# Two MLPs behind an RWKV-7 scan on one core: a new cost model for the planner, a gate on either of two engines, two interleaved blocks

## The chip, the cores and the metric

The kernel runs on one core of a Trainium2 chip. The time is device microseconds from the start of the execution to its end; of several runs the median is taken. The engines are TensorE (PE; its weight loads are shown apart as PEld), VectorE (DVE), ScalarE (ACT), GpSimd (POOL) and SyncE (SP), which here issues all DMAs. Each works through its own list of instructions in a fixed order and waits on semaphores where an input comes from another one.

## The reference

Attention is a recurrence over 768 tokens for 4 x 8 heads of size 40, followed by two MLPs over 3072 tokens with 320 features and 2048 hidden units, each with a squared Relu:

```
for t in range(S):
    y[:, :, t] = einsum('bhd,bhde->bhe', rt, state)
    Sa = einsum('bhde,bhe->bhd', state, at)
    state = state * wt[:, :, None, :] - einsum('bhd,bhe->bhde', Sa, bt)
    state = state + einsum('bhd,bhe->bhde', vt, kt)
x = y as (3072, 320)
x = relu(x @ moe_w_in) ** 2 @ moe_w_out
return relu(x @ moe2_w_in) ** 2 @ moe2_w_out
```

## The kernel before

**Attention** is done in chunks of 32 tokens. There are 12 units of 64 tokens and two halves of the batch, so 24 slots. For two slots at a time `keys` and `invert` prepare the chunk's triangular system: four scans of 520 elements along the decays, transposes on VectorE, and a long chain of small VectorE operations. `values` and `chain` then carry the state from chunk to chunk with many small matmuls in fp32.

**The MLPs** work in 12 blocks of 256 tokens, each in 16 steps `f` of 128 hidden units. A step is an `in_step` (8 matmuls of 256 columns into one of two banks `HB`), a `gate`, and an out step. In the first MLP (`block1`, `out_step1`) the out step has 8 matmuls of 256 columns; in the second (`block2`, `out_step2`) 6 of 320. Values are split into a high and a low part in fp32r, so that three products stand for one: the gate makes Relu (into `m_r`, which lies in the tile `mm`), the square of it, the rounded high part `m_h` and the rest `m_l`. Relu and Square are ScalarE's; `copy(AV, ...)` may go to ScalarE or VectorE, `sub(VG, ...)` to VectorE or GpSimd. `m_h` and `m_l` are rings of three, `m_r` and `HB` of two. The first MLP's block can start when both slots of its unit are done; it is the filler of TensorE during attention.

**The weights** come as 64-bit numbers and are decoded into pairs of fp32r by `halves` and `decode_t` (first MLP, beside the first slots) or `decode` (second MLP, when attention has ended and its memory is free). `halves` has three VectorE operations on U32. The second MLP needs slice `f` of its weights for step `f` of block 0.

**The order** of all of this is worked out by a planner (`_Plan`). Each operation is recorded with its inputs, its outputs and a priority (a lower number goes first): gate -200 and up, blocks' input -100 and up, attention by its slot's number, decoding 2.7, MLP matmuls 1000 and up. `run` simulates the five engines with the durations of `cost` (`array` and `pe_time` for TensorE), always takes the engine that can start first (in a tie VectorE, then ScalarE, GpSimd, TensorE, SyncE), and emits the operation in that order. An operation recorded by `either` goes to the engine that takes it first, but VectorE at first passes over one that another engine would end no more than `BIAS` = 800 ns later (lines 352 to 355). If nothing else is left for it and nothing is due within 300 ns, VectorE takes it all the same (lines 361 to 365). The planner's durations are thus not the chip's; only the order and the engine that it chose are what runs. `self.left` counts the operations with a tag that are still to be emitted; attention's have the tag "att".

An out step of the MLPs has the priority of its in step plus 1.5, so TensorE does in(j), out(j-1), in(j+1), out(j), and a gate has the time of out(j-1) and in(j+1) to finish. `check_w` (16 reductions over the decays, after the fourth block) looks for decays outside a range, for which a general version stands at the end of the program; it doesn't run with these inputs.

Every operation of the planner shows line 69 in the profile, so groups are told apart by their tiles.

Of the kernel before, what the change touches and what calls it, by code (L numbers as in the profile page):

```python
# [26 lines left out]
NF = 16  # L27
# [45 lines left out]
class _Plan:  # L73
# [65 lines left out]
    def cost(self, eng, op, outs, ins):  # L139
        o = outs[0]  # L140
        n = 1
        for _, c in o.ap[1:]:
            n *= c
        if eng == "SP":
            return 690.0 if o.ap[0][1] in (32, 64) else 480.0
        psum = any(str(z.space).endswith("PSUM") for z in ins)
        if eng == "ACT":
            return (55 if psum else 93) + (90 if len(ins) > 1 else 0) + n / 1.2
        if eng == "POOL":
            return 149 + 2.1 * n if ins else 35 + 0.83 * n  # L150
        if op == "reciprocal":
            return 70 + n * 6.25
        if op == "tensor_reduce":
            n = 1
            for _, c in ins[0].ap[1:]:
                n *= c
        if op in ("tensor_copy", "tensor_scalar") and not psum:
            n /= 2
        return (64 + n) / 0.96

# [87 lines left out]
    def array(self, ops):  # L248

        cycles, columns, tiles, mode = 0, 0.0, [], None  # L250
        for _, _, passes, outs, ins, _ in ops:
            k, m = ins[0].ap[0][1], ins[0].ap[1][1]
            n = 1
            for _, c in outs[0].ap[1:]:
                n *= c
            r0, c0 = ins[0].offset // ins[0].ap[0][0], outs[0].offset // outs[0].ap[0][0]
            rows = 32 if k <= 32 else 64 if k <= 64 else 128
            cols = 32 if m <= 32 else 64 if m <= 64 else 128
            if rows == 128:
                r0 = 0  # L260
            mode = (rows, cols)
            if ins[0].dtype == F32R:
                cycles += max(n, 2 * m) + 6
                columns += n * m / 128
                tiles = []
                continue
            tile_ = (r0, c0)
            clash = [z for z in tiles if not (z[0] != r0 or z[1] != c0)] or (
                rows == 128 and any(z[1] == c0 for z in tiles)
            )  # L270
            if tiles and not clash:
                cycles += passes / 2 * m
                columns += passes * n * m / 128
                tiles.append(tile_)
            else:
                cycles += passes * max(n, m)
                columns += passes * n * m / 128
                tiles = [tile_]
        return mode, cycles, columns
# [40 lines left out]
    def run(self, until=None):  # L320
        while until is None or self.left.get(until, 0):
# [20 lines left out]
            if e == "DVE":  # L342
                keep = []
                while avail:
                    z = heapq.heappop(avail)
                    j = z[1]
                    if j in self.done:
                        continue
                    keep.append(z)
                    alts = self.tasks[j][0]  # L350
                    cost = alts[e][1]
                    if any(
                        max(self.free[o], self.ready[j][o], t) + alts[o][1] <= t + cost + BIAS for o in alts if o != e
                    ):
                        continue
                    i = j
                    keep.pop()
                    break
                for z in keep:
                    heapq.heappush(avail, z)  # L360
                if i is None and self.pend[e] and self.pend[e][0][0] < t + 300:
                    self.free[e] = self.pend[e][0][0]
                    continue
# [24 lines left out]
def rwkv7_two_mlp_kernel(  # L388
# [611 lines left out]

    def gate(h, i):
        gg, gh, gl = m_r[i % 2], m_h[i % NG], m_l[i % NG]
        A.activation(out=gg, in_=h, func=AF.Relu)
        A.activation(out=gg, in_=gg, func=AF.Square)
        copy(AV, gh, gg)
        sub(VG, gl, gg, gh.bitcast(F32))

# [84 lines left out]

    obs = [bank[0:2], bank[2:4]]

    def block2(m, at, rows):
        ob = obs[m % 2]
        plan.prio = P_X + m
        load_x(x2a[at].rearrange("p (k t) -> p k t", k=2), x2b[at])
        split_x(m_xh[m % 2], m_xl[m % 2])
        for f in range(NF):  # L1100
            i = m * NF + f
            j = NBLK * NF + i
            plan.prio = P_M + j
            in_step(w2, m_xh[m % 2], m_xl[m % 2], f, HB[i % 2][:, 0:256])
            plan.prio = P_G + j
            gate(HB[i % 2][:, 0:256], i)
            plan.prio = P_M + j + 1.5
            out_step2(w2, f, i, ob)
        plan.prio = P_G + j
        for s in range(2):  # L1110
            o = m_o[s]
            src = ob[s][:, 0:320]
# [27 lines left out]
        V.tensor_reduce(out=wrow[:, 256:257], in_=wrow[:, 0:256], axis=AX.X, op=ALU.max)  # L1140
        V.tensor_copy(out=wbad, in_=wrow[:, 256:257])

    for m in range(NBLK):
        block2(m, m, lambda p, s: orow[p, s, m])
        if m == min(3, NBLK - 1):
            check_w()
    plan.run()
    sched.__exit__(None, None, None)
# [45 lines left out]
    with tc.If(bad > 0):  # L1194
# [3 lines left out]
        plan.run()  # L1198
        with tc.For_i(0, NU) as q:
            block1(0, q)  # L1200
            block2(0, q, lambda p, s: orow[p, s, bass.ds(q, 1)].rearrange("o t d -> (o t) d"))
            plan.run()
        w2x.close()

# [77 lines left out]
```

## Time and profile before

| | |
|---|---|
| median of 3 runs | 1204.93 us (1204.58 to 1208.73) |
| profiled execution | 1209.43 us, span 1207.6 us |
| mean granted TensorE clock | 0.955 |
| busy TensorE, VectorE, ScalarE, GpSimd | 1104.0, 805.9, 747.5, 388.2 us |

The page's second part shows the span in 40 slices of 30.2 us; a digit is the busy share in tenths. [...] A list of waits names the waiting engine and what it wrote to, then the engine and the tile that released it, the sum of the waits, their number and the longest. A group of instructions has the output and input tiles, the shape, the count, the busy time, the mean duration in ns, and the engine's idle time just before them.

### The profile page before, as it was taken

How to read it: one execution, taken by the hardware profiler on the slowest of the kernel's cores; microseconds unless marked ns; L12 is line 12 of the kernel's file. 1: busy time of each engine (PE TensorE's matmuls, PEld its weight loads, DVE VectorE, ACT ScalarE, POOL GpSimd, SP SyncE). 2: the span in 40 equal slices, each digit the busy share in tenths (PEclk: the TensorE clock that was granted, in tenths of full speed). 3: DMA queues.
4: the chain of work that ended last, by engine and by line, in shares of the span. 5: the costliest groups of instructions: out<-in, count | busy, mean ns of one | idle time of the engine just before them, and what ended most of it. 6: DMA issues, size and time to landing. Idle time of an engine off the chain costs nothing.

```text
span 1207.6 us, 43193 instructions
## 1 busy us (share of the span) xinstructions
PE 1104.0 (91%) x18096; PEld 1032.2 (85%) x18096; DVE 805.9 (67%) x1786; ACT 747.5 (62%) x2077; POOL 388.2 (32%) x443
## 2 busy tenths in 40 slices
PE   3888898998989998899899999999899999999996
PEld 2656787887878887798789899999899999999996
DVE  6887888789888978999798746666773232222221
ACT  4496554555565565556446468888666666666664
POOL 7544334223323332343224117776820000000000
PEclk9986789999998999999899999999899999999999
DMA  8555343155325515533451322332241010101000
GB/s 244 143 154 146 85 104 103 57 127 146 79 70 138 136 49 127 143 90 78 123 121 36 60 74 84 93 93 82 79 140 36 25 29 24 33 24 27 13 12 14
DMA packets 142239, 103.86 MB, mean 86 GB/s; under 512 B 98001, under 2 KB 110162, under 8 KB 142034
## 3 DMA queue, kind: packets, MB, share of 16 engines
q1 hardware_dynamic: 142034, 101.00, 31.5%
q8 instruction: 144, 2.36, 0.8%
q14 instruction: 61, 0.50, 0.1%
HBM read 82.88 MB, written 11.80 MB: 78 GB/s over the span
## 4 chain that ended last, share of the span: by engine, by line
PE 50%; DVE 7%; ACT 3%; issue 2%; DMA 1%; POOL 1%; SPq 1%; DVEq 0%; ACTq 0%; POOLq 0%
PE bank L69 50%; DVE mm L69 3%; DVE q L69 2%; ACT mm L69 1%; ACT q L69 1%; SPq L69 1%; DVE x L69 0%; DVE y L69 0%; DVE kt L69 0%; ACT m_h L69 0%; DMA v<-in_el_dram 0%; POOL kb L69 0%; DMA lk<-kt 0%; DVE p L69 0%; DMA mm<-in_win_dram 0%
## 5 line engine op out<-in xcount | busy, mean ns | idle before, releaser
L69 PE MATMUL bank<-m_xh,wi 128*128 128x256 f32 x1920 | 387.0, 286 | 9.7 <-ACT mm L69 5.4
L69 POOL TENSOR_TENSOR m_l<-mm,m_h 128x256 fp32r<-128x256 f32 x200 | 162.8, 816 | 546.3 <-ACT m_h L69 293.7
L69 PEld LDWEIGHTS bank<-m_xh,wi 128*128 128x128 f32 x1920 | 315.3, 193 | 13.2 <-ACT mm L69 6.0
L69 PE MATMUL bank<-m_xl,wi 128*128 128x256 f32 x1152 | 324.2, 285 | 1.8 <-POOL m_xl L69 1.8
L69 ACT ACTIVATE mm<-bank 128x256 f32<-128x256 f32 x384 | 146.2, 382 | 233.1 <-PE bank L69 214.3
L69 DVE TENSOR_TENSOR m_l<-mm,m_h 128x256 fp32r<-128x256 f32 x184 | 85.0, 462 | 217.6 <-ACT m_h L69 209.7
L69 PEld LDWEIGHTS bank<-m_xl,wi 128*128 128x128 f32 x1152 | 222.3, 193 | 2.3 <-POOL m_xl L69 2.3
L69 ACT ACTIVATE mm<-mm 128x256 f32<-128x256 f32 (+3 forms) x500 | 205.0, 423 | 30.6 <-POOL m_xl L69 14.8
L69 PE MATMUL bank<-m_h,wo 128*128 128x256 f32 x960 | 206.7, 297 | 0.1
L69 PE MATMUL bank<-wo,m_h 128*128 128x320 f32 x768 | 172.5, 311 | 1.7 <-ACT m_h L69 1.2
L69 PEld LDWEIGHTS bank<-m_h,wo 128*128 128x128 f32 x960 | 156.6, 192 | 10.0 <-issue 1.4
L69 PE MATMUL bank<-m_l,wo 128*128 128x256 f32 x576 | 156.6, 284 | 0.1
L69 ACT CAST m_h<-mm 128x256 fp32r<-128x256 f32 x359 | 145.1, 405 | 10.2 <-PE bank L69 1.9
L69 PEld LDWEIGHTS bank<-wo,m_h 128*128 128x128 f32 x768 | 125.7, 190 | 2.2 <-ACT m_h L69 1.4
L69 PE MATMUL bank<-wo,m_l 128*128 128x320 f32 x384 | 119.2, 310 | 1.0 <-POOL m_l L69 1.0
L69 DVE TENSOR_TENSOR mm<-mm 128x30 f32<-128x30 f32 (+9 forms) x317 | 106.0, 334 | 8.4 <-ACT wi L69 0.7
L69 PEld LDWEIGHTS bank<-m_l,wo 128*128 128x128 f32 x576 | 110.7, 192 | 0.5 <-POOL m_l L69 0.3
L69 DVE TENSOR_TENSOR q<-bank,cs 32x128 f32<-32x128 f32 (+1 forms) x240 | 87.7, 366 | 30.6 <-ACT q L69 22.2
L69 PE MATMUL bank<-q,lk 128*40 128x72 f32 x1536 | 63.7, 233 | 23.7 <-DVE q L69 10.6
L69 PEld LDWEIGHTS bank<-q,lk 128*40 128x40 f32 x1536 | 53.7, 120 | 31.7 <-ACT mm L69 9.9
L69 ACT COPY q<-bank 40x256 f32<-40x256 f32 (+1 forms) x168 | 54.6, 325 | 37.3 <-PE bank L69 33.6
L69 ACT ACTIVATE q<-bank 32x160 f32<-32x160 f32 x192 | 56.6, 295 | 27.3 <-PE bank L69 24.8
(135 smaller groups left out, 1633.1 us busy)
## 6 DMA issues: line engine op xcount, KB each, us to landing
kb<-in_el_dram SPq DMA_DIRECT2D x24, 512.0 KB
mm<-in_win_dram SPq DMA_DIRECT2D x30, 256.0 KB
a<-in_el_dram SPq DMA_DIRECT2D x24, 256.0 KB
v<-in_el_dram SPq DMA_DIRECT2D x24, 256.0 KB
r<-in_er_dram SPq DMA_DIRECT2D x24, 256.0 KB
lk<-kt SPq DMA_DIRECT2D x96, 64.0 KB
mm<-in_wr_dram SPq DMA_DIRECT2D x20, 260.0 KB
mm<-in_wout_dram SPq DMA_DIRECT2D x20, 256.0 KB
```

The lines of the kernel that those rows point to most:

```text
L69: self.plan.op(self, op, lambda: getattr(self.real, op)(*args, **kw), outs, ins, kw)
```

## The change

It has three parts. The planner's cost of scans, transposes and U32 operations on VectorE is raised, as is that of an fp32r matmul (30 cycles beside its columns for 6). The gate's Relu and Square may go to either ScalarE or VectorE (there Square is the product of the bank and its Relu), and while attention has operations left VectorE's bias against what another engine could do is four times as large for the MLPs' operations. In the second MLP blocks 0 and 1 are interleaved: block 1 begins 5 steps after block 0, and from there their steps take turns. The other ten blocks run one after the other as before; the count `i` of steps, which picks the buffers, now starts from 0 in each of them.

```diff
@@ -154,7 +154,13 @@
-        if op in ("tensor_copy", "tensor_scalar") and not psum:
+        if op == "tensor_tensor_scan":
+            n *= 2.15
+        elif op == "transpose":
+            n = max(1.09 * n, 1.85 * min(n, 512))
+        elif o.dtype == U32:
+            n *= 1.2
+        elif op in ("tensor_copy", "tensor_scalar") and not psum:
             n /= 2
         return (64 + n) / 0.96
@@ -260,7 +266,7 @@
             if ins[0].dtype == F32R:
-                cycles += max(n, 2 * m) + 6
+                cycles += max(n, 2 * m) + 30
@@ -349,8 +355,9 @@
                     cost = alts[e][1]
+                    bias = BIAS * (4 if self.tasks[j][3] != "att" and self.left.get("att", 0) else 1)
                     if any(
-                        max(self.free[o], self.ready[j][o], t) + alts[o][1] <= t + cost + BIAS for o in alts if o != e
+                        max(self.free[o], self.ready[j][o], t) + alts[o][1] <= t + cost + bias for o in alts if o != e
                     ):
                         continue
@@ -1000,8 +1007,14 @@
     def gate(h, i):
         gg, gh, gl = m_r[i % 2], m_h[i % NG], m_l[i % NG]
-        A.activation(out=gg, in_=h, func=AF.Relu)
-        A.activation(out=gg, in_=gg, func=AF.Square)
+        plan.either(
+            lambda: A.activation(out=gg, in_=h, func=AF.Relu),
+            lambda: V.tensor_scalar(out=gg, in0=h, scalar1=0.0, scalar2=None, op0=ALU.max),
+        )
+        plan.either(
+            lambda: A.activation(out=gg, in_=gg, func=AF.Square),
+            lambda: V.tensor_tensor(out=gg, in0=h, in1=gg, op=ALU.mult),
+        )
         copy(AV, gh, gg)
         sub(VG, gl, gg, gh.bitcast(F32))
@@ -1092,21 +1105,25 @@
-    def block2(m, at, rows):
-        ob = obs[m % 2]
-        plan.prio = P_X + m
-        load_x(x2a[at].rearrange("p (k t) -> p k t", k=2), x2b[at])
-        split_x(m_xh[m % 2], m_xl[m % 2])
-        for f in range(NF):
-            i = m * NF + f
-            j = NBLK * NF + i
+    def blocks2(ms, ats, rows):
+        steps = sorted((f + LAG * k, m, f) for k, m in enumerate(ms) for f in range(NF))
+        for i, (_, m, f) in enumerate(steps):
+            if f == 0:
+                plan.prio = P_X + m
+                load_x(x2a[ats[m - ms[0]]].rearrange("p (k t) -> p k t", k=2), x2b[ats[m - ms[0]]])
+                split_x(m_xh[m % 2], m_xl[m % 2])
+            j = (NBLK + ms[0]) * NF + i
             plan.prio = P_M + j
             in_step(w2, m_xh[m % 2], m_xl[m % 2], f, HB[i % 2][:, 0:256])
             plan.prio = P_G + j
             gate(HB[i % 2][:, 0:256], i)
             plan.prio = P_M + j + 1.5
-            out_step2(w2, f, i, ob)
-        plan.prio = P_G + j
+            out_step2(w2, f, i, obs[m % 2])
+            if f == NF - 1:
+                plan.prio = P_G + j
+                finish2(obs[m % 2], lambda p, s: rows(m, p, s))
@@ -1140,9 +1157,11 @@
-    for m in range(NBLK):
-        block2(m, m, lambda p, s: orow[p, s, m])
-        if m == min(3, NBLK - 1):
+    LAG = 5
+    lead = min(2, NBLK)
+    for ms in (range(lead), *([m] for m in range(lead, NBLK))):
+        blocks2(ms, ms, lambda m, p, s: orow[p, s, m])
+        if ms[0] == 3:
             check_w()
```

## Rows read from the trace of the kernel before

**Rows 1.** The page: TensorE's total (and others), and its granted clock in 40 slices.
```profile
PE 1104.0 (91%) x18096; PEld 1032.2 (85%) x18096; DVE 805.9 (67%) x1786; ACT 747.5 (62%) x2077; POOL 388.2 (32%) x443
...
PEclk9986789999998999999899999999899999999999
```

**Rows 2.** Table by stage: stretch, length, busy time of each engine (instructions), clock, DMA, GB/s.
```profile
0.00:40.00 40.00, 17.75 (x351) 13.66 (x355) 29.74 (x54) 18.93 (x50) 26.71 (x37) 1.00 0.79 227
40.00:160.00 120.00, 98.86 (x1650) 80.46 (x1642) 99.88 (x266) 79.13 (x230) 54.99 (x56) 0.82 0.46 123
160.00:676.00 516.00, 470.65 (x11525) 427.77 (x11527) 447.32 (x1017) 289.91 (x837) 167.80 (x190) 0.95 0.40 101
676.00:836.00 160.00, 158.85 (x1908) 154.16 (x1902) 96.98 (x198) 120.39 (x346) 88.09 (x104) 1.00 0.28 80
836.00:869.00 33.00, 28.37 (x195) 27.03 (x195) 23.05 (x41) 25.54 (x72) 24.19 (x29) 0.93 0.29 87
869.00:1198.50 329.50, 329.48 (x2487) 329.08 (x2486) 108.42 (x215) 213.62 (x544) 26.45 (x29) 0.99 0.13 35
```

**Rows 3.** Waits of TensorE's weight loads in 160 to 676 us, longest in total.
```profile
PEld bank L69 <- issue: 21.9, 37, 2.7
PEld bank L69 <- ACT mm L69: 14.4, 13, 2.9
PEld bank L69 <- ACT m_h L69: 6.1, 4, 2.3
```

**Rows 4.** The same table in stretches of 11 us at the second MLP's start.
```profile
836.00:847.00 11.00, 10.42 (x81) 10.39 (x81) 6.71 (x16) 10.36 (x31) 6.57 (x9) 1.00 0.35 104
847.00:858.00 11.00, 11.00 (x86) 11.00 (x86) 6.45 (x11) 8.71 (x24) 8.30 (x11) 1.00 0.23 73
858.00:869.00 11.00, 6.94 (x33) 5.64 (x32) 9.88 (x15) 6.47 (x18) 9.32 (x11) 0.78 0.29 83
869.00:880.00 11.00, 11.00 (x67) 10.89 (x67) 7.68 (x12) 8.26 (x22) 7.30 (x7) 0.76 0.49 136
```

**Rows 5.** VectorE's operations on w_out: ns min/median/max, first and last start in us.
```profile
L69 DVE TENSOR_TENSOR wo<-dt x8: 481/962/1028, 737.5 to 875.6; 128x320 fp32r<-128x320 f32 x8
```

**Rows 6.** Groups of VectorE, whole span: scans, transpose, the decode's U32 pair, a chain's step.
```profile
L69 DVE TENSOR_SCALAR mm<-mm 128x256 uint32<-128x256 uint32 x100 | 37.5, 391 | 6.9 <-ACT mm L69 6.3
...
L69 DVE TENSOR_TENSOR_SCAN mm<-mm,cs 128x520 f32<-128x520 f32 x20 | 25.6, 1279 | 0.2
L69 DVE SCALAR_TENSOR_TENSOR mm<-mm 128x256 uint32<-128x256 uint32 x50 | 24.6, 496 | 0.2
...
L69 DVE TENSOR_TENSOR mm<-mm 128x96 f32<-128x96 f32 x40 | 14.0, 349 | 0.7
...
L69 DVE STREAM_TRANSPOSE tt<-mm 128x512 f32<-128x512 f32 x10 | 11.1, 1107 | 0.2
```

**Rows 7.** Groups of VectorE and ScalarE in the second MLP, 880 to 1200 us.
```profile
L69 DVE TENSOR_TENSOR m_l<-mm,m_h 128x256 fp32r<-128x256 f32 x151 | 64.8, 429 | 189.5 <-ACT m_h L69 188.3 <-POOL m_l L69 0.9
...
L69 DVE TENSOR_TENSOR m_xl<-mm,m_xh 128x768 fp32r<-128x768 f32 x9 | 8.6, 958 | 4.6 <-ACT m_xh L69 4.2
...
L69 DVE COPY mm<-bank 128x320 f32<-128x320 f32 x11 | 5.4, 492 | 15.4 <-PE bank L69 14.1 <-DMA mm<-x2b 1.3
...
L69 DVE CAST m_h<-mm 128x256 fp32r<-128x256 f32 x10 | 2.9, 288 | 1.5 <-ACT mm L69 1.5
...
L69 ACT ACTIVATE mm<-mm 128x256 f32<-128x256 f32 x172 | 70.9, 418 | 4.7
L69 ACT CAST m_h<-mm 128x256 fp32r<-128x256 f32 x162 | 65.8, 406 | 5.0
L69 ACT ACTIVATE mm<-bank 128x256 f32<-128x256 f32 x172 | 65.5, 382 | 99.9 <-PE bank L69 94.6 <-POOL m_l L69 5.3
L69 ACT COPY mm<-bank 128x320 f32<-128x320 f32 x11 | 4.7, 427 | 1.3 <-PE bank L69 1.0
```

**Rows 8.** Groups of VectorE and GpSimd in 160 to 676 us.
```profile
L69 DVE TENSOR_TENSOR m_l<-mm,m_h 128x256 fp32r<-128x256 f32 x11 | 7.6, 695 | 10.5 <-ACT m_h L69 6.0 <-POOL m_xl L69 4.0 <-POOL mm L69 0.5
...
L69 DVE TENSOR_TENSOR mm<-bank,mm 64x256 f32<-64x256 f32 x7 | 2.8, 403 | 2.7 <-ACT mm L69 2.6
...
L69 POOL TENSOR_TENSOR m_l<-mm,m_h 128x256 fp32r<-128x256 f32 x102 | 81.5, 800 | 225.3 <-ACT m_h L69 125.2 <-issue 61.6 <-PE bank L69 19.5
```

More of the change, by code (lines that the diff above doesn't have):

```diff
@@ L1107, in block2, with finish2 @@
             plan.prio = P_M + j + 1.5
-            out_step2(w2, f, i, ob)
-        plan.prio = P_G + j
+            out_step2(w2, f, i, obs[m % 2])
+            if f == NF - 1:
+                plan.prio = P_G + j
+                finish2(obs[m % 2], lambda p, s: rows(m, p, s))
+    def finish2(ob, rows):
         for s in range(2):
@@ L1200, in rwkv7_two_mlp_kernel @@
             block1(0, q)
-            block2(0, q, lambda p, s: orow[p, s, bass.ds(q, 1)].rearrange("o t d -> (o t) d"))
+            blocks2([0], [q], lambda m, p, s: orow[p, s, bass.ds(q, 1)].rearrange("o t d -> (o t) d"))
             plan.run()
```

## The prediction

> **What bounds the kernel now.** I read the page first: TensorE is busy for 1104.0 of 1207.6 us, and the clock granted to it is below full only in the first two thirds [rows 1]. The table by stage then says where TensorE's missing time lies [rows 2]. From 869 us on (second MLP alone) it is busy for 329.48 of 329.50 us, in 676 to 836 us (the rest of the first MLP, with the second MLP's weights decoded beside it) for 158.85 of 160. There is nothing to win in either but a better-fed start. The losses are: 0 to 40 us (the first loads, 22 us idle), 40 to 160 us (attention and the first decode; 21.1 us idle, clock 0.82), 160 to 676 us (attention with the first MLP as filler; 516 - 470.65 = 45.4 us idle, and 0.05 x 516 = 26 us lost to the clock), 836 to 869 us (start of the second MLP; 4.6 us idle, and few matmuls) and the last 9.1 us (output).
>
> In 160 to 676 us VectorE is the fullest engine beside TensorE (447.32 of 516 us), ScalarE has 289.91, GpSimd 167.80 [rows 2]. TensorE's weight loads wait there for no single thing: the largest named waits are for the first MLP's gate (ScalarE's mm and m_h, 14.4 + 6.1 us), and 21.9 us have no releaser in the profile [rows 3]. The filler is plentiful (it lasts until 836 us), so TensorE idles because its fixed order holds an instruction whose input comes later than the planner thought. That is what a corrected cost model can change.
>
> **The change part by part.** The sum is made against the profiled execution, 1209.43 us (span 1207.6). The median of the runs is 1204.93, which is 0.9963 of it; the result is scaled by that at the end.
>
> (a) The two interleaved blocks. In 836 to 847 us TensorE ran 81 matmuls, in 847 to 858 us 86, in 858 to 869 us only 33, and in 869 to 880 us 67 at a clock of 0.76 [rows 4]. From 869 to 1198.5 us the pace is 329.48 / 2487 = 0.1325 us each, so 22 us would hold 166. There were 100: 66 x 0.1325 = 8.7 us lost. The cause is the decode: block 0 wants a slice of w_out and w_in every 14 matmuls (1.855 us), and the last slice is written only at 875.6 + 1.0 us [rows 5]. The gain needs slices to be wanted later than they come. With LAG = 5, slice f (from 5 on) is wanted at step 5 + 2(f - 5): the 16th at step 25. Some 13 steps ran before 869 us (192 less 329.5 / 1.84), so the stage began near 840 us, and the 16th slice is wanted near 840 + 25 x 1.84 = 886 us, 9 us behind its arrival. The cover is that decode speed; were the decode 9 us slower the loss would come back one for one. I take -9 us; bounds -9 and 0. Step numbers now start at 0 in each block, so m_h's ring of three meets itself at a block's edge (15 and 0 are one buffer). The old out step is followed by one in step before the buffer is needed again, so I cost that at nothing; its price if uncovered is one ScalarE cast, 0.406 us [rows 7], at ten edges, 4 us.
>
> (b) The gate on either engine. In the planner's loop VectorE is asked first when engines are equally early, and takes a refused task anyway if nothing else is due within 300 ns. The trace shows what this does to the one gate step that was free to choose so far: m_l went to VectorE 151 times from 880 to 1200 us [rows 7], but 11 times, against 102 on GpSimd, in 160 to 676 us [rows 8]. So in the second MLP nearly the whole gate will move to VectorE, and before 676 us perhaps a tenth of it.
> In the second MLP a gate on VectorE costs: Relu and Square from a bank, 0.403 us each by the nearest row, a two-input op of 64x256 with one input in a bank [rows 8], with 0.288 (a cast without a bank) and 0.492 (a 320-wide copy out of a bank) as ends; the cast 0.288; the subtraction 0.429 [rows 7]. That is 1.52 us (1.29 to 1.70), and dependent VectorE steps follow one another with 0.7 us of idle in 40 [rows 6], so 1.55. TensorE's step is 1.84 us. Today's path is 0.382 + 0.418 + 0.406 + 0.429 = 1.64 us on two engines. The new one is no longer, but 84% of VectorE; a block adds 0.958 (m_xl) and 0.492 (output copy) [rows 7], 1.45 us against 16 x 0.29 = 4.6 us of room. What is queued behind a late VectorE step is the next Relu, and TensorE's out step waits for that. I take +1 us over the stage; bounds 0 and +25 (the 1.70 end, with 0.1 us of handover per step, 1.98 - 1.84 = 0.14 x 179).
> The trace has the copy of 128x320 out of a bank at 427 ns on ScalarE and 492 on VectorE [rows 7]. [...]
> Before 676 us: 11 gates x 0.81 = 9 us go on VectorE, and the fourfold bias takes off it most of the 11 subtractions, 7.6 us [rows 8]. These cancel: 0.
>
> (c) The model. The old formula gives a scan of 520 elements (64 + 520) / 0.96 = 608 ns; it took 1279. The transpose of 512 (tt) 600; it took 1107. The U32 pair of the decode 200 and 333; they took 391 and 496 [rows 6]. An f32r step of the second MLP was planned at (8 x 262 + 6 x 326) / 2.4 = 1.69 us and took 1.855; the new model says 1.83. In 160 to 676 us that is 37 scans x 0.66 = 24 us, 9 transposes x 0.5 = 5 us, about 30 of 447 us of VectorE's work that the plan took to be free, and some 4% on the filler. In the first decode it is 100 x 0.19 + 50 x 0.16 = 27 us of VectorE against 99.88 us busy in 40 to 160 us. VectorE does the same work after the change; what may go is TensorE's waiting. The trace of before can't show a new order. Bounds for 160 to 676 us: at best all 30 us turn into waits that vanish; at worst the new order waits as much more as I hope to win, +9. I take a fifth of the 45.4 us idle, -9: the shift per wait is small (0.5 to 0.7 us), while the named waits last up to 2.9 us each and sit at the gate, which the model hardly touches. For 40 to 160 us I take -3 of the 21.1 us, bounds -10 and +3: there is no filler yet, and VectorE is 83% busy, so a better order has little room.
>
> Sum: 1209.4 - 9 + 1 - 9 - 3 = 1189.4; x 0.9963 = **1185 us**.
>
> **Rivals.**
> 1. The order brings nothing. The waits at the gate and those without releaser [rows 3] are not due to durations. Then only (a) and (b) stay: 1209.4 - 8 = 1201.4, x 0.9963 = 1197 us.
> 2. The order brings much: half of the 45.4 + 26 us lost to idling and clock goes, and 8 us of the first decode. 1209.4 - 8 - 36 - 8 = 1157, 1153 us. For it: VectorE's understated work (30 us) is nearly as large as TensorE's idle time. Against: it waits in many small places.
> 3. Slower: VectorE becomes the bound of the second MLP, after 869 us. It decides as soon as a gate with its share of m_xl and output copy takes over 1.84 us on VectorE, 0.2 us over my sum. At the upper end, 0.14 us on 179 steps = 25 us; with nothing from the order 1209.4 - 9 + 25 = 1225, 1221 us. Against it: the planner hands a Relu to ScalarE when VectorE isn't free; for it: it knows VectorE's bank reads only as 333 ns, and puts four steps of a chain there.
> 4. The new order is worse before 676 us by the +9, and eats (a): 1209.4 - 9 + 1 + 9 = 1210, 1206 us. The mechanism would be GpSimd. An m_l takes 800 ns there [rows 8], and VectorE's own m_l has a mean of 695 ns in that stage [rows 8] against 429 in the stage where GpSimd is nearly still [rows 7]; the fourfold bias sends GpSimd more. [...]
> 5. The change doesn't do what it says: gates stay on ScalarE. Then 0 instead of +1, no other number moves; it is in 1.
>
> **How the numbers follow.** Forecast 0.50 (1175 to 1193 us), rival 1 0.17 (1193 to 1202), rival 2 0.08, rival 3 0.15, rival 4 0.10. A measurement of this kernel can tell about 0.5% (6 us, 1199 to 1211) from no change. Faster: forecast, rival 2 and half of rival 1, 0.66. Same: rival 4 and the rest of rival 1, 0.18. Slower: rival 3, 0.16. The range takes in rival 1, most of 4 and the near part of 2: 1163 to 1210 us, with half of rival 2 and nearly all of 3 outside.
>
> **What would show it.** (a) right: no 11 us stretch with under 75 matmuls where the second MLP begins; wrong: waits for wi or wo there. (b) right: after 900 us VectorE busy 75 to 90%, ScalarE under 25%, TensorE still full; wrong: TensorE below 99% there. (c) right: TensorE idle less than 40 us in the same attention work, with the waits for the gate and the unnamed ones smaller; wrong: attention ends later than 676 us with as much idle time. The prediction fails most likely by (c), whose size rests on a choice of mine, and then by VectorE's unmeasured bank reads.

## The result: slower by half a per cent, and the profile after

The changed kernel takes 1211.16 us (median of 20 runs, 1203.65 to 1222.59), the kernel before 1204.76 in the runs beside it (20 runs): a ratio of 1.0057, 95% interval 1.0036 to 1.0077. One of the 20, the one of 1222.59 us, counts as a slow run and is left out of the ratio. The forecast was 1185 us, 26 us less, and the range ended at 1210.

The profiled executions hide this: 1206.58 us, span 1204.6, against 1209.43 and 1207.6 before. The reason is the granted clock, 0.963 in the one after and 0.955 in the one before; it differs between executions of one kernel, too (0.949 to 0.967 in 19 of the changed one). Span x (1 - clock) books what the clock took, span x clock the rest. The profiled execution before has 54.3 + 1153.3 us, the one after 44.6 + 1160.0. The medians over many runs are 49.2 + 1155.3 (35 later runs of before, beside jit_lat) and 47.1 + 1161.6 (19 of after). So apart from the clock the kernel became 6 to 7 us longer, in the profiles as in the medians, and the stages are to be compared by TensorE's idle time.

The page of the changed kernel, total and granted clock; VectorE has 113 us more, ScalarE 126 less [rows 1]:

```profile
PE 1093.2 (91%) x18096; PEld 1020.8 (85%) x18096; DVE 918.5 (76%) x2061; ACT 621.7 (52%) x1743; POOL 437.2 (36%) x502
...
PEclk9878799998998899999999999999999999999999
```

The table by stage of the changed kernel, in the stretches of [rows 2] (in each row TensorE, its weight loads, VectorE, ScalarE and GpSimd; then the granted clock as a share of its full rate):

```profile
0.00:40.00 40.00, 15.83 (x339) 12.34 (x339) 29.66 (x45) 16.05 (x43) 28.61 (x37) 1.00 0.70 206
40.00:160.00 120.00, 89.71 (x1432) 71.47 (x1432) 94.39 (x260) 75.70 (x221) 53.02 (x53) 0.79 0.46 126
160.00:676.00 516.00, 475.52 (x11649) 435.43 (x11650) 448.90 (x1011) 293.71 (x841) 186.12 (x211) 0.97 0.40 101
676.00:836.00 160.00, 156.95 (x2009) 150.49 (x2008) 106.12 (x219) 114.02 (x323) 83.38 (x96) 1.00 0.29 78
836.00:869.00 33.00, 32.13 (x242) 31.48 (x241) 21.10 (x41) 28.25 (x80) 23.32 (x29) 1.00 0.32 90
869.00:1198.50 329.50, 323.10 (x2431) 319.55 (x2430) 218.33 (x490) 94.01 (x239) 62.74 (x79) 1.00 0.14 38
```

TensorE's idle time against [rows 2]: +1.9 us in 0 to 40, +9.2 in 40 to 160 (30.3 for 21.1), -4.9 in 160 to 676 (40.5 for 45.4), and from 676 us to the end +1.5 (1.9 - 3.8 + 6.4 and 3.0 less after the last mark). Together +7.7. The forecast had -3, -9 and -8 in the last three. So the forecast misses some 14 us up to 160 us, 4 in the long stage and 9.5 from 676 us on, 27.7 together; by the medians it misses 26. In the second MLP the start is now smooth, and the gap stands later. Stretches of 10 us of the changed kernel:

```profile
860.00:870.00 10.00, 9.13 (x67) 8.48 (x67) 7.80 (x12) 7.20 (x21) 8.69 (x11) 1.00 0.34 92
870.00:880.00 10.00, 9.29 (x61) 7.89 (x59) 8.00 (x12) 7.81 (x22) 8.54 (x11) 1.00 0.28 80
880.00:890.00 10.00, 7.21 (x52) 6.52 (x52) 8.02 (x10) 6.04 (x16) 8.25 (x10) 1.00 0.22 63
890.00:900.00 10.00, 9.36 (x68) 9.11 (x69) 8.04 (x11) 5.37 (x14) 3.76 (x5) 1.00 0.62 181
900.00:910.00 10.00, 9.53 (x68) 8.79 (x68) 8.34 (x12) 4.36 (x13) 4.71 (x5) 1.00 0.73 216
910.00:920.00 10.00, 10.00 (x79) 10.00 (x79) 7.66 (x15) 5.84 (x16) 2.23 (x3) 1.00 0.30 95
```

Full pace is 78 matmuls in 10 us (79, then 77). In 860 to 890 us 54 are missing, 6.9 us; in 890 to 910 us, where VectorE has `check_w`'s reductions (1.15 us each), 20, 2.6 us. The operations on w_out and the out steps of both MLPs, by tile (min/median/max ns, first and last start):

```profile
L69 DVE TENSOR_TENSOR wo<-dt x6: 477/1008/1976, 750.0 to 887.9; 128x320 fp32r<-128x320 f32 x6
...
L69 PE MATMUL bank<-m_h,wo x960: 275/280/582, 152.1 to 835.4; 128*128 128x256 f32 x192
...
L69 PE MATMUL bank<-wo,m_h x768: 302/309/417, 837.6 to 1196.2; 128*128 128x320 f32 x192
```

The last slice is written at 887.9 + 1.0 us, not at 876.6 [rows 5]: 12.3 us later. The second MLP's out steps began at 837.6, so it was wanted at 837.6 + 25 x 1.83 = 883.4 (1.83 us a step as in only_inter below, 349.9 us over 191 steps). Of the 12.3 us 8.7 are attention's: the decode's memory is free when attention's last output is stored, at 725.4 us for 716.7. The other 3.6 are the decode's own. The stores, first of the kernel before, then of the changed one:

```profile
L69 SPq DMA_DIRECT2D ys<-y x48: 292/388/1360, 95.6 to 716.7; - x48
```

```profile
L69 SPq DMA_DIRECT2D ys<-y x48: 287/388/1670, 100.8 to 725.4; - x48
```

The slices aren't the only thing that TensorE waited for. The waits of its weight loads in 837 to 912 us:

```profile
PEld bank L69 <- POOL m_l L69: 3.6, 5, 1.5
PEld bank L69 <- ACT mm L69: 3.2, 7, 0.9
PEld bank L69 <- DVE wo L69: 1.6, 2, 1.3
PEld bank L69 <- DVE m_l L69: 0.9, 2, 0.6
```

By name a slice accounts for 1.6 of 9.3 us, the gate for the rest. The longest wait for GpSimd's `m_l` ended at 881.1: its input was there at 877.8, but it stood in GpSimd's fixed list behind another `m_l` and two of the decode's operations and began at 880.2. So part of the loss is the decode's operations between the gate's, and not the time of the slice itself. Had nothing else been late, the last slice would still have been 5.6 us behind its step.

In 40 to 160 us the weight loads' added waits are mostly for GpSimd. The three longest waits for it, first before, then after:

```profile
PEld bank L69 <- POOL m_xl L69: 5.0, 4, 2.5
PEld bank L69 <- POOL kb L69: 2.0, 2, 1.2
PEld bank L69 <- POOL m_xh L69: 1.9, 3, 0.7
```

```profile
PEld bank L69 <- POOL kb L69: 5.8, 3, 3.5
PEld bank L69 <- POOL m_xh L69: 5.4, 4, 3.5
PEld bank L69 <- POOL m_xl L69: 5.3, 3, 2.9
```

That is 16.5 us for 8.9, 7.6 of the 9.2 us. GpSimd has no more work there (53.02 us for 54.99), so TensorE waits not for more work but for work that comes later.

The gate did what was forecast in the second MLP. VectorE's and ScalarE's groups of the changed kernel in 900 to 1200 us:

```profile
L69 DVE TENSOR_TENSOR m_l<-mm,m_h 128x256 fp32r<-128x256 f32 x109 | 46.9, 430 | 43.2 <-ACT m_h L69 40.7
L69 DVE TENSOR_TENSOR mm<-bank,mm 128x256 f32<-128x256 f32 x105 | 44.6, 424 | 3.6
L69 DVE TENSOR_SCALAR mm<-bank 128x256 f32<-128x256 f32 x105 | 44.5, 424 | 46.8 <-PE bank L69 46.8
L69 DVE CAST m_h<-mm 128x256 fp32r<-128x256 f32 x96 | 28.2, 294 | 3.4
```

Relu and Square take 424 ns each for the 403 assumed; 105 of 160 Relus moved, and VectorE waits 46.8 us for TensorE's bank there, so it isn't the bound.

### The profile page after: what moved, and what is told of

Its sections match the earlier page's. It is cut to its first block, busy times and chain, and to the rows that moved or that the text cites. A ratio compares the mean times of both kernels' runs of the same rounds, so it can differ in the third digit from the quotient of the medians.

```text
span 1204.6 us, 43026 instructions
## 1 busy us (share of the span) xinstructions
PE 1093.2 (91%) x18096; PEld 1020.8 (85%) x18096; DVE 918.5 (76%) x2061; ACT 621.7 (52%) x1743; POOL 437.2 (36%) x502
## 4 chain that ended last, share of the span: by engine, by line
PE 44%; DVE 10%; ACT 3%; issue 2%; DMA 2%; POOL 1%; SPq 1%; DVEq 0%; ACTq 0%; POOLq 0%
PE bank L69 44%; DVE mm L69 4%; DVE q L69 2%; ACT mm L69 1%; ACT q L69 1%; SPq L69 1%; DVE y L69 0%; DVE sp L69 0%; DVE cs L69 0%; DMA w<-in_wl_dram 0%; DVE kb L69 0%; ACT m_h L69 0%; DMA dt<-in_nat_dram 0%; POOL m_xl L69 0%; DMA r<-in_er_dram 0%
## 5 line engine op out<-in xcount | busy, mean ns | idle before, releaser
L69 POOL TENSOR_TENSOR m_l<-mm,m_h 128x256 fp32r<-128x256 f32 x244 | 195.1, 801 | 534.5 <-DVE m_h L69 248.8
L69 ACT ACTIVATE mm<-bank 128x256 f32<-128x256 f32 x263 | 100.3, 382 | 312.6 <-PE bank L69 298.1
L69 ACT ACTIVATE mm<-mm 128x256 f32<-128x256 f32 (+1 forms) x386 | 159.3, 425 | 48.8 <-POOL m_xh L69 15.4
L69 DVE TENSOR_TENSOR m_l<-mm,m_h 128x256 fp32r<-128x256 f32 x140 | 69.5, 497 | 67.2 <-ACT m_h L69 61.8
L69 ACT CAST m_h<-mm 128x256 fp32r<-128x256 f32 x275 | 111.1, 405 | 10.4 <-PE bank L69 3.1
L69 DVE TENSOR_TENSOR mm<-mm 128x30 f32<-128x30 f32 (+8 forms) x315 | 103.3, 328 | 9.9 <-ACT wi L69 2.0
L69 DVE TENSOR_SCALAR mm<-bank 128x256 f32<-128x256 f32 x121 | 51.3, 424 | 52.8 <-PE bank L69 52.4
L69 PEld LDWEIGHTS bank<-wo,m_l 128*128 128x128 f32 x384 | 72.1, 188 | 4.7 <-POOL m_l L69 3.6
```

What stands on the lines that cost most here:

```text
L69: self.plan.op(self, op, lambda: getattr(self.real, op)(*args, **kw), outs, ins, kw)
```

## The experiments

First theory: VectorE's truer costs make a worse order (first decode, attention's end), and this takes the interleaving's gain. Rivals: the gate's free choice does it, or any touch of a planner's input redraws the order by as much. The code below shows the lines that matter. The table has all 20 kernels. Columns: ratio to the kernel before; median loss to the clock, span x (1 - clock); then from the profile: TensorE's idle time and clock loss up to 160 us; end of the first decode; attention's last store; length of the second MLP's out steps; how long after it was wanted the 16th slice came (wanted 15 steps of 1.83 us from the start without interleaving, 25 with LAG 5, 29 with LAG 1).

| kernel | ratio | clock loss | 0 to 160 | decode 1 | last store | MLP 2 | late |
|---|---|---|---|---|---|---|---|
| before | 1 | 49.2 | 65.8 | 135.6 | 716.7 | 358.9 | 9.6 |
| after | 1.0057 | 47.1 | 80.1 | 145.4 | 725.4 | 359.0 | 5.6 |
| jit_lat | 1.0028 | 48.9 | 65.3 | 136.2 | 712.2 | 365.9 | 8.6 |
| jit_pe | 1.0025 | 50.7 | 68.6 | 134.4 | 718.3 | 362.5 | 8.9 |
| only_inter | 0.9910 | 46.5 | 61.1 | 132.5 | 713.9 | 349.9 | -5.2 |
| inter_jit | 0.9901 | 39.9 | 66.7 | 133.3 | 710.9 | 350.8 | -2.1 |
| inter_pe | 1.0163 | 60.5 | 79.7 | 142.0 | 708.4 | 350.5 | -44.3 |
| only_gate | 1.0109 | 59.0 | 68.7 | 134.4 | 720.3 | 358.7 | 6.5 |
| gate2 | 1.0003 | 48.2 | 68.3 | 132.8 | 712.6 | 359.5 | 10.2 |
| wo_gate | 1.0068 | 48.0 | 77.9 | 143.4 | 726.0 | 357.6 | 6.7 |
| only_dve | 1.0233 | 77.1 | 83.3 | 150.3 | 736.7 | 379.6 | 27.2 |
| only_scan | 1.0161 | 69.5 | 63.6 | 134.0 | 727.4 | 378.5 | 23.2 |
| only_u32 | 1.0211 | 64.5 | 83.3 | 149.5 | 726.5 | 369.8 | 15.2 |
| u32_jit | 1.0257 | 67.8 | 80.9 | 146.8 | 722.7 | 369.4 | 14.8 |
| wo_dve | 1.0087 | 54.5 | 68.5 | 136.3 | 710.1 | 349.6 | -41.1 |
| wo_scan | 1.0159 | 64.1 | 83.0 | 144.4 | 715.4 | 349.6 | -17.3 |
| wo_u32 | 0.9977 | 52.8 | 78.0 | 138.5 | 725.7 | 350.7 | -6.1 |
| wo_u32_pe | 0.9973 | 51.5 | 70.8 | 137.6 | 719.0 | 361.5 | 13.0 |
| after_jit | 1.0101 | 51.0 | 76.1 | 142.2 | 738.1 | 361.0 | 6.4 |
| after_lag1 | 0.9980 | 45.9 | 77.6 | 143.2 | 730.1 | 352.6 | 0.8 |

**only_inter** is the changed kernel with the gate, the bias and all costs taken back, so that the interleaving stands alone.

```diff
# of the change this alone stays, with blocks2
+    LAG = 5
+    lead = min(2, NBLK)
+    for ms in (range(lead), *([m] for m in range(lead, NBLK))):
+        blocks2(ms, ms, lambda m, p, s: orow[p, s, m])
```

> Only the interleaving of blocks 0 and 1 of the second MLP (with the step count that starts anew in each block). Theory A: the 8.7 us lost between 858 and 880 us come back when the decode is not late: time 0.5 to 0.75% below the kernel before. Rival C (the decode is what limits the start whatever the order, or another wait replaces it): a loss of 6 us or more stays between 860 and 920 us, time within 0.3% of before.

Measured 0.991 (0.9875 to 0.9944), a little more than the first theory expected. The second MLP has no gap; its start in this kernel, in stretches of 10 us:

```profile
850.00:860.00 10.00, 10.00 (x78) 10.00 (x77) 4.70 (x9) 8.22 (x25) 8.16 (x11) 1.00 0.21 67
860.00:870.00 10.00, 10.00 (x77) 9.82 (x77) 8.22 (x12) 8.61 (x24) 9.05 (x11) 1.00 0.23 66
870.00:880.00 10.00, 10.00 (x77) 9.86 (x76) 9.44 (x10) 7.67 (x20) 9.09 (x10) 1.00 0.44 114
880.00:890.00 10.00, 10.00 (x77) 10.00 (x76) 7.59 (x11) 5.97 (x17) 3.45 (x5) 1.00 0.74 218
```

Its decode ends at 877.2 us, its last slice is wanted at 882.5: out steps of 349.9 us for 358.9. Step (a) is worth its 9 us where its cover holds.

**only_gate** is the kernel before with the free choice of Relu's and Square's engine; **gate2** has that in the second MLP alone; **wo_gate** is the changed kernel with ScalarE's gate.

```diff
-        A.activation(out=gg, in_=h, func=AF.Relu)
+        plan.either(
+            lambda: A.activation(out=gg, in_=h, func=AF.Relu),
+            lambda: V.tensor_scalar(out=gg, in0=h, scalar1=0.0, scalar2=None, op0=ALU.max),
+        )
# ... and the Square in the same way
```

> Only the gate's Relu and Square on either engine, in the kernel before; bias and durations as before, blocks one after the other. Theory A: the second MLP stays full (TensorE idle under 2 us after 900 us), time within 0.3% of before. Rival B: VectorE, loaded with gates before 720 us, holds attention up: last store 5 us or more later than 716.7 us and time 0.5% or more above.

> The kernel before with Relu and Square free to go to VectorE in the second MLP alone; the first MLP's gate is ScalarE's as before. Theory (the gate costs nothing in the second MLP itself, what it cost alone came from the order before 840 us): the attention part keeps its order up to the last slots, TensorE is full after 890 us, and the time is within 0.3% of the kernel before, not 1.1% above. Rival B (VectorE's gates in the second MLP or in the decode cost the 13 us): 0.8% or more above.

> The changed kernel with the gate's Relu and Square back on ScalarE alone; interleaving, bias and all new costs stay. If the gate's engines cost what they cost alone (1.1% of the kernel before), it is at 0.995 of the kernel before. If the interleaving is eaten by the VectorE costs whatever the gate does (theory E with G), attention's last store stays at 725 us or later, and the time at 1.003 to 1.02.

only_gate is 1.1% slower (1.0068 to 1.0151), gate2 no different (0.9978 to 1.0028). So in the second MLP the gate is free, as forecast, and what only_gate loses lies ahead of it: the first MLP's last out step begins at 846.2 us for 838.4, with only 6 Relus on VectorE before 680 us (2.5 us of work). The last store was little later (+3.6 us), less than rival B wants. In the changed kernel the gate makes no difference (1.0068 without, 1.0057 with it; last store at 726.0 us): the second of its two cases. So the gate's price alone looks like one of the order that it came into, not of its instructions; no run repeats it in another order.

**only_dve** is the kernel before with VectorE's three new costs; **wo_dve** the changed kernel without them.

```diff
+        if op == "tensor_tensor_scan":
+            n *= 2.15
+        elif op == "transpose":
+            n = max(1.09 * n, 1.85 * min(n, 512))
+        elif o.dtype == U32:
+            n *= 1.2
```

> Only the three new VectorE costs (scans, transposes, U32) are put into the kernel before. Theory A (the new VectorE durations reorder the first 160 us for the worse): TensorE idles about 8 us more in 40 to 160 us than before, attention's last store comes 5 to 9 us later than 716.7 us, and the time is 0.5 to 1.0% above the kernel before. Rival B (the gate and the bias cost it, the durations are harmless): idle time in 40 to 160 us within 3 us of before, last store within 3 us, time within 0.4%. My forecast's step (c) would have it 1% faster.

> The changed kernel with the three VectorE costs taken back to the old ones; gate, bias, TensorE cost and interleaving stay. Theory A: idle time of TensorE in 40 to 160 us falls back from 30 to about 21 us, attention's last store comes before 720 us, and the time is 0.8% or more below the changed kernel (at or below the kernel before). Rival B: it stays at the changed kernel's time, 0.3 to 0.7% above the kernel before.

only_dve is 2.3% slower (1.019 to 1.0276), far more than expected; wo_dve is at 1.0087 (1.0055 to 1.0119), not better than the changed kernel, though one theory had it no slower than the kernel before. So the costs harm alone, but taking them back doesn't give back the time: without them attention ends at 710.1 us, the slices come 41 us early, and the first MLP ends at 854.4 us. How only_dve begins its second MLP, in stretches of 11 us:

```profile
846.00:857.00 11.00, 10.59 (x81) 10.23 (x81) 4.40 (x12) 10.16 (x30) 8.37 (x11) 1.00 0.35 108
857.00:868.00 11.00, 8.21 (x55) 7.34 (x53) 7.96 (x15) 6.31 (x18) 8.61 (x11) 1.00 0.29 81
868.00:879.00 11.00, 5.61 (x19) 4.47 (x19) 9.23 (x15) 7.50 (x20) 7.92 (x10) 0.50 0.36 110
879.00:890.00 11.00, 6.75 (x24) 5.20 (x22) 6.95 (x13) 4.93 (x14) 9.09 (x11) 0.50 0.27 78
890.00:901.00 11.00, 9.30 (x36) 8.21 (x37) 7.57 (x13) 6.42 (x16) 8.50 (x11) 0.50 0.33 82
901.00:912.00 11.00, 11.00 (x80) 11.00 (x80) 7.64 (x11) 6.19 (x17) 3.59 (x4) 0.95 0.61 191
```

19 to 36 matmuls where 86 fit [rows 4]: TensorE runs at the decode's pace (the 16th slice comes 27.2 us late), and the granted clock is 0.50 in these three stretches.

**only_scan** and **only_u32** split these costs, on the kernel before; **wo_scan** and **wo_u32** take the same lines out of the changed kernel.

```diff
# only_scan; wo_scan takes these out
+        if op == "tensor_tensor_scan":
+            n *= 2.15
+        elif op == "transpose":
+            n = max(1.09 * n, 1.85 * min(n, 512))
# only_u32; wo_u32 takes these out
+        if o.dtype == U32:
+            n *= 1.2
```

> Of the change, only the costs of scans and transposes in the kernel before (the U32 cost stays old). Theory G (dearer scans make the planner hold VectorE for fuller, so it gives more of attention's own products to GpSimd, where they take 1.2 to 1.3 us, and VectorE waits for them): products of kb, x and p on GpSimd in 160 to 680 us rise from 47 by 10 or more, attention's last store comes at 725 us or later, time 1% or more above before. Rival H (it is the decode's U32 cost in the first 160 us): store within 5 us of 716.7, time within 0.5%.

> Of the change, only the cost of U32 operations on VectorE in the kernel before. Rival H: the first MLP's decode and attention's first slots come out later, first store of attention at 100 us or later for 95.6, last store at 725 us or later, time 1% or more above before. Theory G: last store within 5 us of 716.7, time within 0.5% of before.

> The changed kernel with the scan and transpose costs taken back; the U32 cost stays. If those costs are what moves attention's end (only_scan 727.4, wo_u32 725.7 us): last store at 720 us or earlier. The U32 cost still lengthens the second MLP's decode (from attention's end to its last slice 160 us or more; 151 without it in wo_u32), and the first 160 us stay at a loss of 75 us or more. Time 0.995 to 1.01 of the kernel before.

> The changed kernel with the U32 cost alone taken back; scan and transpose costs stay. Theory S: the loss up to 160 us falls from 80 to 70 us or less, the decode ends before 135 us, while attention still ends at 722 us or later through the scan cost; time at 0.993 to 1.00 of the kernel before. Theory D: no such pairing, loss up to 160 us of 75 us or more.

Both harm alone, where each theory had one of them harmless: 1.0161 (1.0106 to 1.0217) and 1.0211 (1.0162 to 1.0259), at different places. The costs of scans and transposes move attention's end: 716.7 to 727.4 us (before, only_scan), 715.4 to 725.4 (wo_scan, after), 726.5 to 736.7 (only_u32, only_dve), some 10 us in each pair. One pair alone would prove little, for after_jit, a touch that means nothing, moves that store by 12.7 us (725.4 to 738.1). Theory G's way there is seen in two of the three: attention's products kb, x and p on GpSimd in 160 to 680 us rise from 42 (not 47, as the expectation has it) to 56 in only_scan and from 50 to 62 from only_u32 to only_dve, but only from 46 to 47 from wo_scan to after. The first MLP ends earlier in return (838.4 to 827.5; 858.7 to 835.4): filler and attention change places. So wo_scan, expected at no more than 1.01, came out at 1.0159 (1.0125 to 1.0194): attention early, first MLP late.

The U32 cost lengthens both decodes. Five pairs of kernels differ by it alone (before and only_u32, jit_lat and u32_jit, only_scan and only_dve, wo_dve and wo_scan, wo_u32 and after). In all of them the first decode ends later with it, by 7 to 16 us, and the second, from the last store to the last slice, takes 12 to 22 us more. In only_u32 the first ends 14 us later (135.6 to 149.5). only_u32's first two stages, for [rows 2]:

```profile
0.00:40.00 40.00, 16.63 (x351) 12.63 (x355) 28.72 (x47) 17.77 (x46) 27.50 (x36) 1.00 0.75 218
40.00:160.00 120.00, 93.68 (x1414) 75.65 (x1407) 92.66 (x253) 74.45 (x216) 53.70 (x50) 0.72 0.46 121
```

VectorE is less busy there than before (92.66 for 99.88 us), TensorE idles 5 us more, and its clock is 0.72 for 0.82. In the second decode after and wo_u32 compare best, for they have the same last store (725.4 and 725.7 us), and wo_u32's last slice is started at 875.9 on GpSimd, 12 us earlier:

```profile
L69 DVE TENSOR_TENSOR wo<-dt x5: 1009/1019/1022, 749.2 to 873.8; 128x320 fp32r<-128x320 f32 x5
L69 POOL TENSOR_TENSOR wo<-dt x3: 891/898/945, 842.5 to 875.9; 128x320 fp32r<-128x320 f32 x3
```

With that the interleaving works again (350.7 us), and the ratio is 0.9977 (0.9955 to 0.9998). after's long decode isn't for lack of VectorE. In 726 to 876 us, the table by stage of the changed kernel and then of wo_u32:

```profile
726.00:876.00 150.00, 148.19 (x1207) 145.98 (x1206) 97.93 (x168) 124.90 (x352) 106.15 (x123) 1.00 0.31 89
```

```profile
726.00:876.00 150.00, 148.78 (x1220) 147.49 (x1219) 109.85 (x183) 128.83 (x362) 113.91 (x132) 1.00 0.33 95
```

With the truer cost VectorE, ScalarE and GpSimd all have more idle time: the order makes them wait. wo_u32's first 160 us stayed at 78.0 us of loss, though, where a fall to 70 was expected.

**inter_pe** is only_inter with the new cost of an fp32r matmul; **wo_u32_pe** is wo_u32 without it.

```diff
-                cycles += max(n, 2 * m) + 6
+                cycles += max(n, 2 * m) + 30
```

> The interleaved blocks and the new TensorE cost of an fp32r matmul (30 cycles for 6) in the kernel before; gate, bias and VectorE costs as before. The interleaving alone was at 0.991 of the kernel before. If the truer TensorE cost is worth what step (c) of the forecast hoped for, 0.98 to 0.985; if it is harmless, 0.991; if it moves attention's end later, as the VectorE costs do, 1.00 or more.

> The changed kernel with both the U32 cost and the TensorE cost taken back; scans, transposes, gate, bias and interleaving stay. If each of the two alone lengthens the first 160 us (only_u32 83 us of idle and clock loss, inter_pe 80, before 66), so that taking the U32 cost alone back left it at 78: now 70 us or less, first MLP's decode ended before 136 us. Attention still ends at 722 us or later. If it stays at 75 or more, it is neither of them but scans, bias or gate in this company, and stays open.

inter_pe is 2.5% slower than only_inter (1.0163, 1.0119 to 1.0208), and in another way than expected: attention ends early (708.4 us), the first MLP late (860.5), and the first 160 us lose 79.7. Taking the cost out of wo_u32 brings these to 70.8 and the first decode's end to 137.6 us, both just short of what was expected, and attention's end to 719.0, earlier than expected. But the time stays (0.9973, 0.9946 to 0.9999): the first MLP ends at 822.3 us, so the slices are wanted earlier and come 13 us late.

**after_lag1** is the changed kernel with the two blocks interleaved almost from the start, so that the last slice is wanted 4 steps later.

```diff
-    LAG = 5
+    LAG = 1
```

> The changed kernel with LAG 1 for 5: the two blocks take turns from the second step on, so that the last slice of the second MLP's weights is wanted at step 29 and not at step 25, 7 us later. Theory E (the interleaving was eaten because the decode, begun 9 us later, ended at 888.9 us, 5 us after the step that wants its last slice): 4 to 9 us less lost in 840 to 910 us, time 0.3 to 0.7% below the changed kernel. Rival F (what stalls there is VectorE's gates and reductions, not the slices): time within 0.2% of the changed kernel.

0.998 (0.9952 to 1.0008), 0.8% under the changed kernel's ratio. The out steps take 352.6 us though the decode ends even later (896.2 us), 0.8 us after its last slice is wanted (5.6 in the changed kernel). So what the interleaving lost hangs on when the slices are wanted against when they come, as theory E has it; it is no fixed price of VectorE's gates and reductions (rival F). The 0.8% are under twice the largest effect of a mere redraw, which follows.

**jit_lat** and **jit_pe** change a number of the planner that means nothing, as a gauge of luck; **after_jit**, **inter_jit** and **u32_jit** do jit_lat's edit on the changed kernel, only_inter and only_u32.

```diff
# jit_lat, after_jit, inter_jit, u32_jit
-    LAT = {"DVE": 127.0, "ACT": 143.0,
+    LAT = {"DVE": 127.0, "ACT": 144.0,
# jit_pe
-                cycles += max(n, 2 * m) + 6
+                cycles += max(n, 2 * m) + 7
```

> The kernel before with one number of the planner moved by next to nothing: its latency behind a ScalarE operation is 144 ns for 143. No operation, engine choice or cost of the change is in it. Theory D (any touch of the planner draws a new order of the first 700 us, and orders differ by 1% in time whatever the reason for the touch): the time moves by 0.5% or more, either way, with TensorE's idle and clock loss in 40 to 680 us moved by 5 us or more. Rival A (the changes of order that cost time came from what the new durations and the gate do): the time stays within 0.4% of before.

> The kernel before with the planner's cost of an fp32r matmul raised by one cycle (7 beside the columns for 6; the change goes to 30). Theory D: the time moves by 0.5% or more, either way, and by another amount than with the ScalarE latency. Rival A: within 0.4% of before.

> The changed kernel with the planner's latency behind a ScalarE operation at 144 ns for 143, as in jit_lat. Theory S (the truer costs do the harm by what they say, whatever the order's luck): attention's last store at 722 us or later, the first MLP's decode ends (last wi out of a bank) at 138 us or later, time at 1.003 to 1.02 of the kernel before. Theory D (luck of the order): each of these moves back to the values of before (716.7 and 132.7 us), and the time differs from the changed kernel's by over 1%.

> Interleaved blocks alone, with the latency at 144 ns for 143. Theory S: the interleaving keeps its gain in another order, 0.990 to 0.997 of the kernel before (the latency alone was at 1.003), the second MLP takes 350 us. Theory D: its gain was luck, 1.00 or more.

> The U32 cost alone with the latency at 144 ns for 143. Theory S: TensorE's idle and clock loss up to 160 us is again 12 us or more above before's 65, the first MLP's decode ends at 140 us or later, time at 1.015 or more. Theory D: the loss up to 160 us is within 5 us of before, time below 1.01.

Each touch gives another order: the last store moves by 1.6 to 12.7 us. The time moves by 0.28% (ratio 1.0004 to 1.0053) and 0.25% (0.9999 to 1.005) on the kernel before, less than the 0.5% of theory D, by 0.4% on the changed one (1.0101, 1.0078 to 1.0125), by 0.1% on only_inter and 0.45% on only_u32. The gain of the interleaving (0.9901, 0.9875 to 0.9926) and the loss of the U32 cost (1.0257, 1.0228 to 1.0285) are there in the redrawn order too, so these two aren't luck. The other effects of 1 to 2.5% (scans, TensorE's cost, the gate alone) weren't repeated so; they are two to six times the largest redraw seen. The changed kernel's own 0.6% is near the size of a redraw.

## Why the prediction was wrong, point by point

Two terms failed. The -3 us of step (c) for the first decode was +9.2 us of idle time in 40 to 160 us, and +1.9 before it; and the -9 us of step (a) was eaten, because (c)'s new order also moved the decode that (a) rests on. From 676 us on TensorE's idle time is 1.5 us more, where -8 was forecast.

**What bounds the kernel**: right in the main. The order decides, and the losses moved among the stages named. But the text takes 676 us as attention's end. In the trace of before attention goes on to its last store at 716.7 us, and it is this time, not 676, that the second MLP's decode waits for.

**(a)** The mechanism and its size were right (only_inter 0.991, -9 us), as was the step at which the last slice is wanted (886 us forecast, 883.4 from the start measured). What failed is its cover. The text says "were the decode 9 us slower the loss would come back one for one"; the decode ended 12.3 us later. In the table the second MLP's out steps take about 350 us wherever the slices come in time, and 353 to 380 where they come 1 to 27 us late; after's 359.0 is 350 + 6.9 (860 to 890 us) + 2.6 (890 to 910 us, where `check_w` runs), less rounding; the sign that the text gave, a stretch with under 75 matmuls, is there. TensorE waited there for the gate behind the decode's operations more than for slices by name. The error is one of method: the sum kept the arrival at 876.6 us from the trace of before while step (c) changed the order that sets it. By the planned -9 of step (c) the decode would have come earlier; the bound of (a), -9 to 0, did hold.

**(b)** +1 us in the second MLP was right: gate2 is at 1.0003, TensorE is busy for the whole of 910 to 920 us and beyond, rival 3 (VectorE the bound) is out. From 900 to 1200 us VectorE's forecast 75 to 90% is 64% (193.3 of 300 us), because only two thirds of the gates moved; ScalarE is at 25% (74.7 us). The +25 us of rival 3 stands on 1.98 us a step, which 1.70 and 0.1 us of handover don't add up to; this didn't move the forecast. "0 before 676 us" was wrong for the gate alone (only_gate +1.1%), and right in the company of the rest (wo_gate). A step that only adds a choice still redraws the plan.

**(c)** This step failed, as the text feared, but in another place than it looked. For 160 to 676 us -9 was taken, -4.9 of idle time measured (40.5 us left, with under 40 as the sign); the whole loss of the stage, with clock, falls to 56 us from 71 in the profile. The waits of TensorE's weight loads in this stage after the change, for [rows 3], are nearly as long as before in sum:

```profile
PEld bank L69 <- issue: 20.4, 33, 2.0
PEld bank L69 <- ACT m_h L69: 11.9, 8, 1.8
PEld bank L69 <- ACT mm L69: 8.1, 8, 2.4
```

20.4 + 11.9 + 8.1 = 40.4 us for 42.4: the longest of each kind fell (2.7, 2.9 and 2.3 us to 2.0, 2.4 and 1.8), but what left the wait for `mm` went to the wait for `m_h`. For 40 to 160 us the text took -3 with bounds -10 and +3, and measured +9.2 of idle time, +1.9 more before 40 us. The bound was the mis-sized term: it took from "VectorE is 83% busy" that little could change, in either direction. What grew was the wait for GpSimd, which the text didn't look at there. And attention's end was left out of the sum: the text names "attention ends later" as a sign of failure, but as much idle time with it. It ended 8.7 us later with less idle time. TensorE's time went to the first MLP instead, whose last out step begins 3 us earlier (835.4 for 838.4). That made up for nothing: the second MLP's weights wait for attention.

**The rivals.** Rival 4 (worse before 676 us, eating (a), 1206 us) came nearest in time. Its mechanism, GpSimd under the larger bias, isn't shown: its `m_l` rose only from 102 to 112, at 820 ns for 800, and the bias wasn't run alone. Why VectorE's `m_l` takes longer in 160 to 676 us (695 ns before, 627 after) than in the second MLP (429 and 430) no run shows. Where the rival put the loss, 160 to 676 us, there was none. Where the waits for GpSimd did grow, in 40 to 160 us, GpSimd had no more work.

**What stays open** is why truer durations make a worse order. The runs show that each of the three new costs does so alone or beside the interleaving, at which place, and that engines wait rather than work. They don't add up: in the company of the rest only the U32 cost harms (0.9977 without it, 1.0057 with it), TensorE's makes no difference (0.9973 and 0.9977), and taking the scans' cost out makes the time longer (1.0159). That the planner's priorities and bias were chosen with the old durations, so that a dearer operation is in effect given less urgency, would fit; it is argued, not shown.

The best kernel of these is the interleaving alone: 1195.68 us, 0.991 of before (0.9901 with the latency touched).

## What to carry to other kernels

When a kernel's order comes from a planner, a truer cost is a new order, not a better one: find the event that the next stage waits for (here attention's last store, then the decode) and watch its time rather than the summed idle time. A gain of the form "wanted later than it comes" has to be checked against what the rest of the change does to the arrival, and two terms that share such an event can't be summed. Before an effect under half a per cent is believed, touch the planner with a number that means nothing: here that alone was worth up to 0.45%.

## What the runs showed of the hardware

TensorE's mean granted clock isn't a property of the kernel alone: in 19 runs of the changed one it lies between 0.949 and 0.967 (spans of 1219.0 and 1205.2 us). Its records in the profiled executions of before and after have two values only, 1.0 and 0.5. In only_dve it was low where the fewest matmuls ran: 1.00 while 81 and then 55 ran in 11 us, 0.50 in the three stretches with 19 to 36, and 0.95 in the first with 80 again. Of only_dve's 28 us, all are booked to the clock (77.1 us for 49.5 beside it), none to the rest. This does not say that the clock caused them: at half clock, half of a wait for a slice is booked so, too. Waits that come with a low clock are best read by their length and not by this split.

VectorE's Relu of 128x256 out of a bank took 424 ns in the changed kernel (mean of 105 in 900 to 1200 us), ScalarE's 383 (55 there).
